# Five blocks of a chunked retention layer with their causal halves on partition halves

## Chip, cores and metric

One core of one Trainium2 chip runs the whole kernel. The metric is the device time of one execution in microseconds (us), as the median of the runs shown.

## The reference

Inputs are q, k, v of 4 batches x 8 heads x 768 tokens x 64. For each batch and head a 64 x 64 state is carried along the tokens, `state = gamma_h * state + k_t v_t^T`, and `y_t = q_t . state / 8`. The outputs of the eight heads side by side make 3072 rows of 512. Each row then goes to one of 8 experts: its normalized product with the normalized expert rows, over `tau`, chooses the expert by argmax and gives the gate (softmax). The expert is `relu(x @ w1[e]) @ w2[e]`, with w1 512 x 1024 and w2 1024 x 512, times the gate.

## The kernel before

**Retention in blocks.** A block m is 256 tokens of one batch for all heads; there are 12, three to a batch (c = m mod 3). A block has two halves u of 128 tokens. Scaling q by gamma^t and k by gamma^-t turns the recurrence into plain products: within a half, scores K Q^T under a causal mask, times V; from earlier tokens, q times the summed state. One loop turn of the program, here step m, does:

- `scores` (L381): per half, 8 products of a 64 x 128 key tile with 128 queries (each matmul is two instructions, fp32), into PSUM banks taken in turn by `pt_` (four banks b0 to b3). `masks` (L402) multiplies them by the 0/1 mask on VectorE, two operations of 512 elements a half.
- `inter` (L453): queries times state, for the halves that have a state.
- `state(m + 1)` (L410): keys times values of the next block, added up in PSUM; for c = 2 only the first half is needed. `state_copy` (ScalarE) and `state_sums` (VectorE) bring it to SBUF.
- the router's logits of block m - 1, and the transposes of the next block's keys and queries, in the order k0, q0, q1, k1. Each is copied from PSUM by ScalarE.
- `intra` (L460): masked scores times values, one half after the other. The outputs of half u stand in bank py0 or py1 (for c > 0).
- `take` (L465): ScalarE copies the outputs, three copies.

Values have to lie as 128 tokens of one half on 128 partitions, while they are loaded with two tokens to a partition. `spread_v` (L395) therefore copies them between partition halves, four copies a block: on ScalarE right after `take` of the step before, and on GpSimd for blocks 10 and 11. Keys are not spread: `state` takes them 64 partitions at a time.

**GpSimd** scales keys and queries of block m + 2 in step m (`scale_ahead`, L867; `scale_k`, L347; `scale_q`, L341), four operations, bound behind the first mask of step m. In steps 4 and 7 the queries are bound behind the router's marks (`mark`, at the end of the step) instead. A transpose of queries needs both query scalings.

**The order** on each engine is written out by hand in the loop at L878; the engines work in that order, with semaphores between them. SP issues all plain transfers in order, with eight semaphores in turn, so that an issue also waits for the landing of the one eight before it. In step m it issues q, k and v of block m + 3 and the output rows of block m - 1 (`rows`, four transfers of 32 partitions). k waits for `state(m + 1)`, v for the second transpose of queries. Query, key and scaled tiles have three buffers, value tiles four.

**The router** works in four groups of three blocks. Steps 3, 6 and 9 choose experts (`pick`); steps 4 and 7 (and 9 and 10 for the third group) rank the tokens and make marks for a table of token positions, which a matmul (`table`) gathers in steps 5, 8 and 10. After step 11 the experts run one after the other, with split fp32 products; the rows of the first are gathered from step 10 on.

Of the kernel before, what the change touches and what calls it, by code (L numbers as in the profile page):

```python
# [38 lines left out]
NG = 4  # L39
CAPS = (416, 408, 400, 392, 384, 380, 360, 356)  # L40
# [21 lines left out]
def _layout():  # L62
    at, n = {}, 0
    for name, w in (("tq", NCB * 2 * H), ("tk", NCB * 2 * H), ("e16", NE), ("tok", 3),
                    ("cols", NE * NG), ("high", NB), ("rest", NB), ("edges", NG - 1), ("quarters", Q),
                    ("ovthr", NOV), ("caps", NE), ("order", NE)):
        at[name] = (n, n + w)
        n += w
# [8 lines left out]
def _constants():  # L77
# [16 lines left out]
    put("tk", (g ** -t).reshape(P, -1))  # L94
    put("e16", (np.arange(NE) / 16.0)[None, :])
# [11 lines left out]
    c16 = np.concatenate([p[:, None] < p[None, :], np.broadcast_to(p[None, :], (P, P))], 1)  # L107
# [4 lines left out]
def retention_moe(ctx: ExitStack, tc: tile.TileContext, q, k, v, emb, tau, w1, w2, const, const16, out):  # L112
# [7 lines left out]
    cst16 = cp.tile([P, 2 * P], FP16, name="cst16")  # L120
    tri, iota = cst16[:, :P], cst16[:, P:]
# [193 lines left out]
    for i in range(3):  # L315
        qin.append(wp.tile([P, 2, 8, D], F32, name="whi"))
        kin.append(wp.tile([P, H, 2, D], F32, name="wlo"))
    for i in range(4):
# [5 lines left out]
    xge = ap_.tile([P, len(EROWS), XW], F32, name="xge", bufs=1)  # L324

# [8 lines left out]

    def load_k(m, h=slice(0, H)):
        return load(kin[m % 3], k, m, h)

    def load_v(m, h=slice(0, H)):
        return load(vin[m % 4], v, m, h)
# [11 lines left out]

    kTs, qTs, yTs, Ss, pst, tBs = {}, {}, {}, {}, [None, None], {}
# [5 lines left out]
    def copy_k(m, s, ps, copy=nc.scalar.copy, js=slice(0, KT)):  # L358
        if m not in kTs:
            kTs[m] = ap_.tile([P, KT, 2, 2, 64], F32, name="kT")  # L360
        return copy(out=kTs[m][:, js, :, s], in_=ps.rearrange("p (j u c) -> p j u c", j=KT, u=2)[:, js])
# [29 lines left out]
    vs = {}  # L391

    pms = {}

    def spread_v(m, u, copy=nc.scalar.copy):  # L395

        if m not in vs:
            vs[m] = ap_.tile([P, 2, H, D], F32, name="vs")
        i = [copy(out=vs[m][s * 64:(s + 1) * 64, u], in_=vin[m % 4][u * 64:(u + 1) * 64, :, s]) for s in range(2)]
# [10 lines left out]
    def state(m):  # L410

        if m % NCB == 0:
            for u in range(2):
                pst[u] = bank(f"pst{u}").rearrange("p (j c) -> p j c", j=KT)
        for j in range(KT):
            for sk in range(2):
                for u in range(1 + (m % NCB < NCB - 1)):
                    for a in range(2):
                        r = slice(u * 64, (u + 1) * 64)
                        h = 2 * j + a  # L420
                        i = nc.tensor.matmul(pst[u][a * D:(a + 1) * D, j, :D], ks_r[r, m % 3, sk, h, :], vin[m % 4][r, h, sk, :],  # L421
# [24 lines left out]
    def y_product(m, u, j, a, lhsT, rhs):  # L446
# [4 lines left out]
        nc.tensor.matmul(pys[m][b][o * D:(o + 1) * D, j], lhsT, rhs, start=first, stop=True, skip_group_check=True)  # L451
# [8 lines left out]
    def intra(m, u):  # L460
        for j in range(KT):
# [1035 lines left out]
```

## Time and profile before

| what | us |
|---|---|
| runs shown | 394.85, 393.69, 394.06; median 394.06 |
| profiled execution | 395.05, with a span of 393.3 |
| steps 1, 2, 3 begin | 19.28, 27.59, 35.90 |
| steps 4 to 8 begin | 44.00, 52.52, 61.04, 69.14, 77.66 |
| steps 9 to 11 begin, retention ends | 86.18, 94.84, 103.46, 108.95 |

The span runs from the first to the last instruction; the profiled execution's own time is 1.75 longer. A step begins with its first score product. Engines: PE is TensorE, PEld its weight loads, DVE VectorE, ACT ScalarE, POOL GpSimd, SP the engine that issues transfers ("SPq" its queue). A row of the order of time gives start and length of a run of like instructions, with the idle time of the engine before it and what ended that in brackets. The granted TensorE clock was 1.00 in all stretches before 200 us, its upper level of 2.4 GHz.

### The profile page before, as it was taken

The page shows a single profiled execution, that of the slowest core. Times are in us where ns is not written, and L with a number is a line of the kernel's source. Part 1 is how long each engine was busy: PE and PEld are TensorE (multiplying, and loading weights), DVE is VectorE, ACT ScalarE, POOL GpSimd, SP SyncE. Part 2 cuts the span into 40 slices and gives each one's busy share as a digit, 9 for nine tenths or more (in the row PEclk, how much of TensorE's full clock was granted, in tenths as well). Part 3 has the DMA queues.
Part 4 walks back from the last instruction along what each step waited for, and adds up shares of the span by engine and source line. Part 5 has one row for each costly group of instructions (what it writes and reads, how often), then busy time and mean ns, then how long its engine had stood idle before and what let it go on. Part 6 is the DMA issues. An engine that isn't in the chain of part 4 may idle for free.

```text
span 393.3 us, 9709 instructions
## 1 busy us (share of the span) xinstructions
PE 384.4 (98%) x3750; PEld 356.7 (91%) x3750; DVE 245.8 (62%) x562; ACT 220.4 (56%) x390; POOL 143.2 (36%) x156
## 2 busy tenths in 40 slices
PE   8999999999999999999999999999999999999993
PEld 7888888888889988999999999999899889999971
DVE  4656787679999568617753862775477447576400
ACT  3488787787674266537446653744765545453420
POOL 2865446267646404224402711520481151001131
PEclk9999999999999999999999999999999999999997
DMA  8999989889588796795959778796988688933121
GB/s 228 295 302 260 255 225 295 235 245 239 158 249 234 221 261 208 240 236 204 320 183 249 252 260 182 243 329 194 254 290 299 163 280 249 216 122 95 31 101 52
DMA packets 86471, 88.03 MB, mean 224 GB/s; under 512 B 9184, under 2 KB 65120, under 8 KB 86416
## 3 DMA queue, kind: packets, MB, share of 16 engines
q1 hardware_dynamic: 81936, 74.32, 66.8%
q0 software_dynamic: 4304, 12.93, 9.9%
q8 instruction: 31, 0.51, 0.6%
q14 instruction: 24, 0.20, 0.2%
q10 hardware_dynamic: 176, 0.07, 0.1%
HBM read 65.00 MB, written 18.43 MB: 212 GB/s over the span
## 4 chain that ended last, share of the span: by engine, by line
PE 80%; DMA 6%; issue 5%; SPq 3%; POOL 2%; DVE 2%; POOLq 0%; ACT 0%
PE pst L247 10%; PE py L451 9%; PE b L247 9%; PE py L1143 8%; PE py L247 7%; PE b L387 6%; PE b L1143 5%; PE pst L1143 4%; PE b L1187 4%; PE py L1187 4%; PE pst L421 3%; PE b L356 3%; PE b L374 3%; SPq L1155 3%; DMA xd<-x 2%
## 5 line engine op out<-in xcount | busy, mean ns | idle before, releaser
L233 DVE TENSOR_TENSOR wlo<-raw,whi 128x1024 fp32r<-128x1024 f32 x60 | 73.0, 1220 | 17.7 <-ACT whi L228 12.2
L1169 POOL DMA_INDIRECT out_dram<-og,si x28 | 30.3, 1082 | 124.8 <-ACT og L1162 74.0
L228 ACT CAST whi<-raw 128x1024 fp32r<-128x1024 f32 x64 | 66.1, 1042 | 0.4 <-DMA raw<-in_moe_w_dram 0.3
L664 POOL DMA_INDIRECT xr<-xd,gi x24 | 30.6, 1276 | 21.0 <-issue 19.5
L1123 DVE STREAM_TRANSPOSE xt<-xg 128x384 f32<-128x384 f32 (+1 forms) x28 | 15.7, 578 | 35.5 <-DMA xg<-xs 35.5
L407 DVE TENSOR_TENSOR pm<-b,mask 128x512 f32<-128x512 f32 x48 | 29.8, 683 | 12.8 <-PE b L387 12.8
L247 PE MATMUL pst<-xh,whi 128*128 128x380 f32 (+7 forms) x96 | 32.1, 334 | 0.0
L247 PE MATMUL pst<-xh,wlo 128*128 128x380 f32 (+7 forms) x96 | 32.0, 333 | 0.0
L247 PE MATMUL pst<-xl,whi 128*128 128x380 f32 (+7 forms) x96 | 31.9, 333 | 0.0
L350 POOL TENSOR_TENSOR hl<-wlo,cst 128x512 f32<-128x512 f32 x22 | 22.5, 1042 | 20.2 <-DVE pm L407 13.0
L1116 ACT CAST xh<-xt 128x408 fp32r<-128x408 f32 (+6 forms) x28 | 14.2, 510 | 25.5 <-DVE xt L1123 25.2
L345 POOL TENSOR_TENSOR hh<-whi,cst 128x512 f32<-128x512 f32 x22 | 22.5, 1044 | 13.6 <-issue 13.6
L273 POOL TENSOR_TENSOR r<-r,half 128x4 f32<-128x4 f32 (+1 forms) x9 | 9.0, 999 | 50.6 <-DVE r L272 50.6
L247 PE MATMUL b<-xh,whi 128*128 128x408 f32 (+7 forms) x80 | 26.8, 335 | 0.0
L247 PE MATMUL b<-xl,whi 128*128 128x408 f32 (+7 forms) x80 | 26.7, 333 | 0.0
L247 PE MATMUL b<-xh,wlo 128*128 128x408 f32 (+7 forms) x80 | 26.6, 332 | 0.0
L247 PE MATMUL py<-xh,whi 128*128 128x288 f32 (+7 forms) x80 | 26.3, 329 | 0.0
L247 PE MATMUL py<-xl,whi 128*128 128x288 f32 (+7 forms) x80 | 26.3, 328 | 0.0
L247 PE MATMUL py<-xh,wlo 128*128 128x288 f32 (+7 forms) x80 | 26.2, 328 | 0.0
L387 PE MATMUL b<-qT,kT 64*128 64x128 f32 x384 | 25.2, 279 | 0.5 <-DVE hl L350 0.5
L253 ACT ACTIVATE hh<-pst 128x380 fp32r<-128x380 f32 (+7 forms) x24 | 11.6, 484 | 24.1 <-PE pst L247 24.1
L387 PEld LDWEIGHTS b<-qT,kT 64*128 64x128 f32 x384 | 22.5, 187 | 2.7 <-issue 1.2
(260 smaller groups left out, 1041.8 us busy)
## 6 DMA issues: line engine op xcount, KB each, us to landing
raw<-in_moe_w_dram SPq DMA_DIRECT2D x60, 512.0 KB
whi<-in_q_dram SPq DMA_DIRECT2D x24, 256.0 KB
wlo<-in_k_dram SPq DMA_DIRECT2D x11, 512.0 KB
xd<-x SPq DMA_DIRECT2D x44, 128.0 KB
xs<-xr SPq DMA_DIRECT2D x6, 768.0 KB
whi<-in_v_dram SPq DMA_DIRECT2D x6, 512.0 KB
wlo<-in_v_dram SPq DMA_DIRECT2D x6, 512.0 KB
xg<-xs SPq DMA_DIRECT2D x16, 192.0 KB
```

Source lines behind the costliest of these rows:

```text
L228: nc.scalar.copy(out=hv, in_=rv)
L233: i = eng.tensor_tensor(out=lv, in0=rv, in1=hv.bitcast(F32), op=ALU.subtract)
L247: nc.tensor.matmul(acc[:, :w], a[:, f], x[:, kt, cols], start=(n == 0), stop=(n == 3 * KT - 1))
L345: return eng.tensor_tensor(out=qs_r[:, m % 3, :, a], in0=qin[m % 3][:, a], in1=w, op=ALU.mult)
L350: return eng.tensor_tensor(out=ks_r[:, m % 3, s, h], in0=kin[m % 3][:, h, s], in1=w[:, h], op=ALU.mult)
L387: nc.tensor.matmul(psc[a][:, j], kTs[m][a * D:(a + 1) * D, j, u].rearrange("p s c -> p (s c)"), q_cols(m, a, j, u), start=True, stop=True, ...
L407: o.append(nc.vector.tensor_tensor(out=pm, in0=psc[a], in1=w, op=ALU.mult))
L451: nc.tensor.matmul(pys[m][b][o * D:(o + 1) * D, j], lhsT, rhs, start=first, stop=True, skip_group_check=True)
L664: return nc.gpsimd.indirect_dma_start(out=xr[:n, j, :], out_offset=None, in_=xd[:rows_, :], in_offset=bass.IndirectOffsetOnAxis(ap=gi[:n, ...
L1143: nc.tensor.matmul(acc[:, :c], a[:, f], x[:, kt, :c], start=(n == 0), stop=(n == 3 * FT - 1))
L1169: i = nc.gpsimd.indirect_dma_start(out=out[:, :], out_offset=bass.IndirectOffsetOnAxis(ap=si[:n, e, j:j + 1], axis=0), in_=og[:n, j, :], i ...
L1187: nc.tensor.matmul(acc[:s, :], x[:, kt, at], a, start=(n == 0), stop=(n == 3 * FT - 1))
```

## The change

It concerns blocks 4, 5, 7, 8 and 10 (`CAUSAL`). Quarter n = 2u + f of 64 tokens is the earlier (f = 0) or later (f = 1) half of half u. Keys and values of these blocks are loaded by quarters, 32 partitions each, in four transfers instead of one; quarter (u, f) goes to 32 partitions of partition half f xor u. Each partition holds two tokens.

- **Keys:** `own_k` scales the token that already lies right, for all 128 partitions; `other_k` scales the other one, 32 partitions at a time, into the neighbouring 32 partitions. That is six operations on GpSimd where there were two.
- **Values:** the same move by `spread_v` (four copies of 32 partitions; ScalarE). It is done one step earlier for all blocks, after `take` of step m - 2; for block 10 it is no longer on GpSimd. The values live in `vx`, three buffers, for all blocks; a causal block's load waits for the values of the block three before it, and is issued at the end of step m.
- **Scores:** `split_scores` does, for each quarter of keys, all 128 queries (f = 0) or only the 64 later ones (f = 1), as 64 x 64 tiles in a written order of the quarters. The zeroed quarter (later keys, earlier queries) is neither computed nor read.
- **Masks:** `split_masks`, four operations of 256 elements a half instead of two of 512, with two new fp16 masks.
- **Values' products:** first the later queries, all 128 keys; then the earlier queries, 64 keys. Both halves u in each.
- **State:** 128 keys a product, half as many products; it stands behind the transposes now, ahead of `intra`.
- Keys of block m + 3 are issued with the queries, behind the first mask. In step 9 the output rows of block 8 and a state sum change place. The router's marks get tiles of their own.

```diff
+CAUSAL = (4, 5, 7, 8, 10)
...
+    vx = [hp.tile([P, H, 3, D], F32, name="xh"), hp.tile([P, H, 3, D], F32, name="xl"),
+          ap_.tile([P, H, 3, D], F32, name="vx", bufs=1)]
...
+    def quarters(src, m, dst):
+        b, c = divmod(m, NCB)
+        o = []
+        for n in range(4):
+            u, f = divmod(n, 2)
+            r = (f ^ u) * 64 + u * Q
+            t = c * T2 + n * 64
+            o.append(nc.sync.dma_start(out=dst(u, slice(r, r + Q)),
+                                       in_=src[b, :, t:t + 64, :].rearrange("h (p s) d -> p h s d", s=2)))
+        return o
...
+            return quarters(k, m, lambda u, r: kin[m % 3][r])
...
+            return quarters(v, m, lambda u, r: vx[m % 3][r, :, u:u + 2])
...
+    def own_k(m, u):
+        return nc.gpsimd.tensor_tensor(out=ks_r[:, m % 3, u], in0=kin[m % 3][:, :, u], in1=weights_k(m, u, slice(0, P)), op=ALU.mult)
+
+    def other_k(m, u, f, eng):
+        r = f * 64 + u * Q
+        o = f * 64 + (1 - u) * Q
+        return eng.tensor_tensor(out=ks_r[o:o + Q, m % 3, u], in0=kin[m % 3][r:r + Q, :, 1 - u],
+                                 in1=weights_k(m, 1 - u, slice(r, r + Q)), op=ALU.mult)
...
+    def split_scores(m):
+        psc = [[pt_().rearrange("p (j g q) -> p j g q", j=KT, g=NQ) for a in range(2)] for u in range(2)]
+        for turn in ((0, 0, 0), (0, 1, 0), (0, 1, 1), (0, 0, 1), (0, 1, 2), (0, 1, 3), (0, 0, 2), (1, 0, 0),
+                     (0, 0, 3), (1, 0, 1), (1, 1, 0), (1, 1, 1), (1, 0, 2), (1, 1, 2), (1, 1, 3), (1, 0, 3)):
+            u, f, j = turn
+            n = f ^ u
+            part = LATER if f else slice(0, Q)
+            for a in range(2):
+                nc.tensor.matmul(psc[u][a][n * 64:(n + 1) * 64, j, :, part], kTs[m][a * D:(a + 1) * D, j, u, n],
+                                 q_cols(m, a, j, u)[:, :, part], start=True, stop=True, skip_group_check=True)
+        return psc
...
+            for r, part in ((slice(0, P), LATER), (slice(u * 64, u * 64 + 64), slice(0, Q // 2))):
+                wr = w[r, :, part].unsqueeze(1).broadcast_to([r.stop - r.start, KT, NQ, Q // 2])
+                o.append(nc.vector.tensor_tensor(out=t[r, :, :, part], in0=psc[a][r, :, :, part], in1=wr, op=ALU.mult))
...
+        for f in range(2):
+            r = f * 64 + u * Q
+            o = f * 64 + (1 - u) * Q
+            i.append(copy(out=x[o:o + Q, :, 2 * u], in_=x[r:r + Q, :, 1]))
...
+        if m in CAUSAL:
+            for u in range(1 + (m % NCB < NCB - 1)):
+                for j in range(KT):
+                    for a in range(2):
+                        h = 2 * j + a
+                        nc.tensor.matmul(pst[u][a * D:(a + 1) * D, j, :D], ks_r[:, m % 3, u, h, :], vx[m % 3][:, h, 2 * u],
...
+            part = slice(0, Q // 2) if u else LATER
+            for j in range(KT):
+                for a in range(2):
+                    for n in range(2):
+                        r = slice(n * 64, n * 64 + 64) if u else slice(0, P)
+                        y_product(m, n, j, a, vx[m % 3][r, 2 * j + a, 2 * n],
+                                  pms[a, n][r, j].rearrange("p (g q) -> p g q", q=Q)[:, :, part], part)
...
+            elif keys:
+                for u in range(2):
+                    after(own_k(m + 2, u), i)
+                for u in range(2):
+                    for f in range(2):
+                        after(other_k(m + 2, u, f, nc.gpsimd), i)
...
         if m and m + 3 < NM:
-            for j in load_q(m + 3):
+            o = load_k(m + 3)
+            for j in (*load_q(m + 3), *(o if m + 3 in CAUSAL else [o])):
                 after(j, i)
...
-            if nxt:
-                i = state(m + 1)
+            if nxt and m + 1 not in CAUSAL:
+                state(m + 1)
                 state_copy(m + 1)
-                if m + 3 < NM:
-                    after(load_k(m + 3), i)
...
+                if m + 1 in CAUSAL:
+                    state(m + 1)
+                    state_copy(m + 1)
+                    state_sums(m + 1)
                 intra(m, 0)
...
         take(m)
-        if m < NM - 2:
-            if m < NM - 3:
-                spread_v(m + 1, 0)
-                spread_v(m + 1, 1)
+        if m + 3 in CAUSAL:
+            load_v(m + 3)
+        for n in range(m + 2 if m else 1, m + 3 if m < NM - 3 else 0):
+            spread_v(n, 0)
+            spread_v(n, 1)
```

## Rows read from the trace of the kernel before

**Rows 1.** Page, part 1: busy time, share of the span, instructions, by engine.
```profile
PE 384.4 (98%) x3750; PEld 356.7 (91%) x3750; DVE 245.8 (62%) x562; ACT 220.4 (56%) x390; POOL 143.2 (36%) x156
```

**Rows 2.** Busy time by step; columns: stretch, length, engines, clock, DMA share, GB/s.
```profile
19.28:27.59 8.31, 8.31 (x155) 7.37 (x154) 5.09 (x11) 6.96 (x13) 6.81 (x7) 1.00 1.03 310
...
44.00:52.52 8.52, 8.52 (x161) 7.57 (x161) 5.48 (x16) 6.91 (x12) 2.04 (x2) 1.00 0.95 252
...
61.04:69.14 8.10, 8.10 (x179) 7.09 (x178) 6.22 (x17) 6.12 (x11) 4.05 (x4) 1.00 1.09 295
...
94.84:103.46 8.62, 8.62 (x162) 7.65 (x161) 8.34 (x27) 6.29 (x10) 3.85 (x6) 1.00 0.82 188
```

**Rows 3.** Chain that ended last, in order of time: start, us, what.
```profile
37.89 0.60 PE py L451 x16
38.48 0.93 PE pst L421 x64
...
44.00 1.99 PE b L387 x32
45.98 1.03 PE py L451 x32
47.02 0.92 PE pst L421 x32
47.94 0.57 PE b L498 x8
48.51 0.59 PE b L356 x4
...
50.62 1.90 PE py L451 x32
...
99.94 0.25 PE b L620 x6
```

**Rows 4.** VectorE in order of time, steps 4 and 5: start, us.
```profile
48.95 0.39 DVE L434 TENSOR_TENSOR s<-pst,tB 128x256 f32<-128x256 f32 x1
...
53.43 1.06 DVE L610 TENSOR_SCALAR xh<-cst,low 128x128 f16<-128x128 f16 x6
...
54.41 2.48 DVE L407 TENSOR_TENSOR pm<-b,mask 128x512 f32<-128x512 f32 x4
```

**Rows 5.** GpSimd in order of time, steps 3, 5 and 9.
```profile
38.12 2.04 POOL L350 TENSOR_TENSOR hl<-wlo,cst 128x512 f32<-128x512 f32 x2 [4.44 <-DMA wlo<-in_k_dram]
...
54.98 2.04 POOL L345 TENSOR_TENSOR hh<-whi,cst 128x512 f32<-128x512 f32 x2 [6.99 <-issue]
...
92.12 2.59 POOL L399 COPY vs<-whi 64x512 f32<-64x512 f32 x4
```

**Rows 6.** GpSimd by groups of instructions: busy us, mean ns, idle before.
```profile
L345 POOL TENSOR_TENSOR hh<-whi,cst 128x512 f32<-128x512 f32 x22 | 22.5, 1044 | 13.6 <-issue 13.6
...
L399 POOL COPY vs<-whi 64x512 f32<-64x512 f32 x6 | 3.7, 609 | 0.3
```

**Rows 7.** ScalarE in order of time, steps 1 and 5.
```profile
21.11 2.52 ACT L399 COPY vs<-wlo 64x512 f32<-64x512 f32 x4
24.47 0.58 ACT L361 COPY kT<-b 128x512 f32<-128x512 f32 x1 [0.83 <-ACT vs L399]
...
25.97 0.62 ACT L361 COPY kT<-b 128x512 f32<-128x512 f32 x1
...
52.57 1.17 ACT L473 COPY yT<-py 64x512 f32<-64x512 f32 x2 [0.29 <-PE py L451]
```

**Rows 8.** VectorE in order of time, steps 9 and 10.
```profile
93.96 0.20 DVE L567 TENSOR_TENSOR rs<-b,oh 128x48 f32<-128x48 f32 x1
...
98.59 1.35 DVE L610 TENSOR_SCALAR xh<-cst,low 128x128 f16<-128x128 f16 x6
```

**Rows 9.** SP's queue in order of time: issues of keys and of weights.
```profile
31.60 0.40 SPq L328 DMA_DIRECT2D wlo<-in_k_dram  x1
...
88.79 4.85 SPq L201 DMA_DIRECT2D raw<-in_moe_w_dram  x8
```

More of the change, by code (lines that the diff above doesn't have):

```diff
@@ L106, in _constants @@
     put("order", np.arange(NE)[None, :])
-    c16 = np.concatenate([p[:, None] < p[None, :], np.broadcast_to(p[None, :], (P, P))], 1)
+    n = np.arange(P)
+    seen = [64 * (blk // 2 ^ u)[:, None] + (2 * row + blk % 2)[:, None] <= (n // Q + 4 * (n % Q))[None, :] for u in range(2)]
+    c16 = np.concatenate([p[:, None] < p[None, :], np.broadcast_to(p[None, :], (P, P)), *seen], 1)
     return c.astype(np.float32), np.ascontiguousarray(c16.astype(np.float16))
@@ L119, in retention_moe @@
     cst2 = cp.tile([P, _CW - _C1], F32, name="cst2")
[L120 to L121 removed]
+    cst16 = cp.tile([P, 4 * P], FP16, name="cst16")
+    tri, iota = cst16[:, :P], cst16[:, P:2 * P]
     ident = cp.tile([P, P], F32, name="ident")
@@ L317, in retention_moe @@
         kin.append(wp.tile([P, H, 2, D], F32, name="wlo"))
+    vat = {m: i % 4 for i, m in enumerate(m for m in range(NM) if m not in CAUSAL)}
     for i in range(4):
@@ L450, in y_product @@
         begun.add((m, b, o))
-        nc.tensor.matmul(pys[m][b][o * D:(o + 1) * D, j], lhsT, rhs, start=first, stop=True, skip_group_check=True)
+        t = pys[m][b][o * D:(o + 1) * D, j].rearrange("p (g q) -> p g q", q=Q)[:, :, part]
+        nc.tensor.matmul(t, lhsT, rhs, start=first, stop=True, skip_group_check=True)
     def inter(m):
@@ L868, in scale_ahead @@
         if m + 2 < NM:
-            for s in range(2 * keys):
-                after(scale_k(m + 2, s), i)
+            if keys and m + 2 not in CAUSAL:
+                for s in range(2):
+                    after(scale_k(m + 2, s), i)
+            elif keys:
[4 more added lines that the diff above has]
+                        after(other_k(m + 2, u, f, nc.gpsimd), i)
             for s in range(2 * queries):
@@ L936, in retention_moe @@
             if urgent:
-                rows(m - 1, x=rows_turn(m - 1, (1,), x))
+                rows(m - 1)
             if nxt:
-                if m < NM - 3:
+                if m + 1 not in CAUSAL and m < NM - 3:
                     state_sums(m + 1)
@@ L956, in retention_moe @@
                 i = transpose_q(m + 1, 1)
-                if m + 3 < NM:
+                if m + 3 < NM and m + 3 not in CAUSAL:
                     after(load_v(m + 3), i)
```

58 lines of the change are left out of this document (38 added, 20 removed).

## The prediction, made before the changed kernel was run

> **What bounds the kernel now.** I read the busy shares first, then the busy time by step, the chain that ended last, and the single engines' order of time. TensorE is busy 98% of the span; VectorE 62%, ScalarE 56%, GpSimd 36% [rows 1]. By step, TensorE has no gap in the four retention steps shown, while VectorE fills 8.34 of 8.62 us in step 10 and ScalarE 6.96 of 8.31 in step 1 [rows 2]. So matmul time saved is saved only where the next engine's list still ends first. The chain runs through TensorE in the retention steps, with no wait between its pieces [rows 3].
>
> Two prices come out of the chain. The products with the state run as 64x64 tiles, four side by side: 32 instructions take 1.03 us, 16 take 0.60 [rows 3]. Sixteen more are four more in a row on each tile, so a 128-column instruction costs 0.43/4 = 0.107 us and entering the shape costs 0.60 - 0.43 = 0.17. The state's 64 instructions of 64 columns, same shape, take 0.93: 16 in a row at 0.107/2 give 0.86. I use 0.107, 0.053 and 0.17. "Sn" is the start of step n.
>
> **The change, part by part.**
> *Scores* of a causal block: 1.99 us now [rows 3]. New, each tile has 4 products (8 instructions) of 128 and 4 of 64 columns: 8 x 0.107 + 8 x 0.053 = 1.28; the written order makes a tile wait once for 0.11: 1.39. With 0.17 behind an ordinary block's values, 1.56 (blocks 4, 7, 10), otherwise 1.45 with 0.06 of pipeline edge (5, 8). At two tiles side by side it would be 2.57, the bound above. I take four, as the products with the state show. Those follow in the same shape, so 1.03 becomes 0.87.
> *Values*: 1.90 now. Later queries: 16 in a row x 0.053 = 0.86; earlier ones, four tiles: 0.43 + 0.17. Sum 1.46, or 1.62 where no state product of their shape stands ahead.
> *State*: 128 rows at a time, 16 x 0.053 + 0.17 = 1.02 for 0.93; for blocks 5 and 8, which need one half only, 0.43 + 0.17 = 0.59 for 0.92. Behind it the values enter their shape free (-0.17).
> By step: 3, 6, 9 save 0.08 each; 4 and 7 save 0.43 + 0.16 + 0.33 + 0.44 = 1.4 each; 5 and 8 save 0.54 + 0.16 + 0.28 = 1.0 each; 10 saves 0.87. **TensorE: 5.9 us less.** Steps 4 and 5 would last 7.1 and 7.5 where they now last 8.52 each.
>
> What takes it back, in order:
> *ScalarE, step 1.* Step 0 now spreads two blocks' values instead of one: four more copies, 2.52 us [rows 7]. The idle 0.83 before the key copy at 24.47 goes; the copies that ended at 25.97 + 0.62 = 26.6 end at 28.3. The scores of step 2 need them and stood at 27.59: **0.8 lost**.
> *Output copies.* Ordinary blocks finish one bank of outputs half-way through their values, so ScalarE's first copy (0.58) ends before the step and the other two 1.17 + 0.1 after the step's start, at 52.52 [rows 3, 7]. A causal block finishes both banks at the end: 0.1 + 0.58 + 1.17 + 0.05 = 1.9 after S5. The products with the state arrive at 1.45, do one bank's first few, and wait: **0.45 lost in each of steps 5 and 8**. Before scores of 1.99 it costs nothing; that margin is 0.1.
> *VectorE.* Four masks take 2.48, 0.62 apart for 512 elements; 256-element operations take 0.39 to 0.41 singly, 0.35 in a row [rows 4]. Eight masks: 2.83, +0.35 a causal step. Step 4's list (masks, router transpose, ranks, output transposes, state sum, marks) ends at 53.43 + 1.06, S4 + 10.5, now [rows 4]; VectorE is idle for 3.0 of the 8.52 us of step 4 [rows 2], and as TensorE comes earlier some of that closes: I get S4 + 9.5. Step 5's masks then start 2.4 after S5; each bank is free as TensorE comes to it. Cost 0, and if that cover goes, some 0.5 a step.
> *GpSimd* is the term that decides. Two scalings take 2.04 us, 1.02 each [rows 5]. A causal block has six for the keys, two over 128 partitions and four over 32, and two for the queries. No row has a product over 32 partitions. The nearest is the copy over 64 between partition halves: 0.61 long, four in 2.59, one after the other [rows 5, 6]. Bounds: 0.26 (a quarter's share) to 1.02 and a gap of 0.1. I take 1.02, because the copies show no overlap and all partitions go in parallel anyway. So 8 x 1.02 = 8.16 a block, where it was 4.08.
> In steps 4 and 7 the queries are scaled behind the marks. Mark end S4 + 9.5, the 0.5 seen between 54.49 and 54.98, and 2.04 give S4 + 12.05 = S5 + 4.95, about when TensorE turns block 6's queries: no loss. Behind it block 7's keys end at S5 + 11.05 and its queries at S5 + 13.1. Step 5 lasts 7.5 + 0.45; step 6 turns queries after 1.99 + 0.60 + 0.57 + 0.59 = 3.75, at S5 + 11.7: **1.4 lost**. Block 8's end 8.16 later, at S5 + 21.25. Step 6 is 8.1 long [rows 2], less 0.08, plus the 1.4; step 7 turns queries after 1.56 + 0.87 + 0.57 + 0.59 = 3.6, at S5 + 20.95: **0.3 lost**. Step 9 repeats step 6 with block 10: **1.4 lost**. Behind the waiting turn stand the key copies, the state and all of the next step on TensorE.
> *Step 10.* TensorE's product with the marks starts at 99.94, just when the marks end (98.59 + 1.35) [rows 3, 8]. From the ranks (93.96) VectorE takes 5.98 to there, +0.35 = 6.3. TensorE now needs only 0.86 + 1.56 + 0.87 + 0.93 + 0.57 + 0.59 = 5.4 from its count: **0.9 lost**. That eats step 10's saving.
> *SP and the transfers.* Keys and values come in four issues each instead of one. One issue takes 0.40 for 512 KB; eight of 128 KB take 4.85, 0.6 each [rows 9]. Six more a causal block are 3.6 us on SP, in steps 1, 2, 4, 5 and 7. Keys go out earlier now; causal values go behind the end of step m and are spread at the end of step m + 1, a whole step later. About 2.4 for the four issues and 6.5 for the landing (keys issued at 31.60 were waited for until 38.12 [rows 5, 9], the longest wait of its kind) just fit the 7.1 + 1.9. Cost 0; without that cover ScalarE's queue stands on the spread, 1 to 2 us in each of steps 5 and 6.
> The Trainium skill (DMA: Bandwidth & Descriptors, Rules for kernel authors) says not to split a transfer over partition halves, since the pieces serialize on the same engines: it speaks against this part, and by it the loads gain nothing, as I count.
>
> Sum: -5.9 + 0.8 + 0.9 + 1.4 + 0.3 + 1.4 + 0.9 = -0.2 us. The work after step 11 is unchanged and starts with its end, so it shifts as a whole. Against the profiled execution, 395.05 (span 393.3 and 1.75 around it), that is 394.85; the median of the runs shown is 394.06, 1.0 lower, so 393.9.
>
> **The rivals.**
> *B, the quarter scalings overlap.* The four touch different partitions; if two run side by side they cost 2.04 for 4.08. Block 7's queries are ready by S5 + 11.0, before 11.7, and the 3.1 us of waits for GpSimd go: 390.8. For it: two 1.04 us scalings fill 2.04 [rows 5, 6], so one already starts a little before the other ends. Against: the copies at 92.12 do not overlap.
> Consecutive GpSimd instructions are no barrier between its eight cores, each of which goes on when its own 16 partitions are done, says the Trainium skill (GPSIMD Engine Reference, 2.1 Instruction dispatch). By that rule B holds; the copies' row does not agree.
> *C, slower: GpSimd's instructions wait for each other.* A quarter scaling overwrites what a whole one wrote, so waits may be set between them. 0.1 on each of eight is 0.8 a block: the waits grow to 2.2, 1.1 and 2.2, and 394.1 + 2.2 = 396.3. It decides from about 0.06 an instruction. For it: the copies stand 0.65 apart at 0.61 long. Against: the pairs of scalings show none.
> *D, all engines keep up.* Only ScalarE's 0.8 is lost: 389.0. Against it stands every list above.
> *E, it does not do what it says:* the four tiles run as two, and scores get longer. GpSimd sets the pace in steps 5 to 9 anyway, so the waits shrink by about as much: 394 to 395, counted with A.
>
> **How the numbers follow.** A measurement here tells about 0.3%, 1.2 us. A (the sum, 392.9 to 395.0 by 0.05 us either way on a scaling and 0.5 on VectorE's lists) has 0.40: 0.30 within the bound, 0.06 below, 0.04 above. B 0.29, faster. D 0.07, faster. C 0.24, slower. So faster 0.42, same 0.30, slower 0.28. The likeliest case gives 393.9. The range 390.2 to 396.6 holds A, B and C at the prices worked out, and leaves out D and the far ends.
>
> **What would show it.** Right: scores near 1.4 to 1.6 and values near 1.5; GpSimd back to back from step 5 to 7; TensorE's turns of queries in steps 6 and 9 waiting over 1 us for GpSimd's query scaling; scores of step 2 waiting 0.8 for ScalarE; the marks' product waiting in step 10. Wrong: a quarter scaling well under 1 us, causal steps of 7.1 us with no wait, or a wait for a value load.

## The result, and the profile after

The changed kernel takes 397.81 us in the median of ten runs (395.86 to 399.81), the kernel before 394.56 on the same chip: a ratio of 1.0075, with a 95% interval of 1.0046 to 1.0104. The forecast was 393.9 (390.2 to 396.6): its likeliest single case was no change, while its chances added up to 0.42 for faster, 0.30 for the same and 0.28 for slower. It is slower, by 0.75%, and outside the range. Ratios here leave disturbed runs out, so they differ a little from quotients of medians. The profiled execution took 397.88, its span 396.2.

Page of the changed kernel, part 1, to set beside [rows 1]:

```profile
PE 382.3 (97%) x3942; PEld 352.7 (89%) x3942; DVE 250.2 (63%) x582; ACT 222.2 (56%) x394; POOL 157.4 (40%) x172
```

TensorE is busy 2.1 us less than before and yet the span is 2.9 longer: it stands still for longer. Busy time by step, columns as in [rows 2], for steps 1, 4 to 6 and 9 to 11:

```profile
18.96:28.12 9.16, 8.37 (x155) 7.36 (x154) 5.09 (x11) 8.92 (x17) 6.78 (x7) 1.00 1.07 298
...
44.53:52.30 7.77, 7.64 (x213) 6.57 (x215) 5.93 (x18) 6.31 (x11) 4.62 (x5) 1.00 0.92 243
52.30:61.25 8.95, 8.08 (x267) 7.15 (x256) 7.82 (x25) 6.69 (x12) 6.55 (x7) 1.00 0.79 211
61.25:69.70 8.45, 8.32 (x150) 6.97 (x149) 6.28 (x17) 6.70 (x12) 8.10 (x9) 1.00 0.73 208
...
86.08:95.48 9.40, 8.89 (x156) 7.18 (x158) 7.22 (x23) 6.81 (x12) 8.11 (x8) 1.00 1.00 280
95.48:105.07 9.59, 8.23 (x226) 7.02 (x225) 8.69 (x30) 5.84 (x9) 2.44 (x4) 1.00 0.85 205
105.07:111.57 6.50, 6.10 (x105) 4.74 (x106) 5.61 (x9) 4.32 (x6) 5.23 (x4) 1.00 0.65 180
```

Length minus TensorE's busy time is its standstill: 0.8 us in step 1, 0.9 in step 5, 0.5 in step 9, 1.4 in step 10, 0.4 in step 11. Steps 4 and 7 gain 0.75 each on [rows 2]; steps 5, 6, 9, 10 and 11 lose 0.4, 0.35, 0.7, 1.0 and 1.0. What TensorE waited for between 18 and 118 us (us in total, times, longest):

```profile
PE b L445 <- issue: 1.3, 1, 1.3
PE py L531 <- issue: 1.1, 2, 0.9
PE b L429 <- ACT kT L403: 0.8, 1, 0.8
PE b L416 <- POOL hh L371: 0.5, 1, 0.5
PE py L531 <- ACT yT L562: 0.3, 1, 0.3
```

The kernel before has not one line in this view. The first two say "issue": the profile shows nothing that TensorE waited for. In its order of time they stand inside step 5's products with the state and inside step 10's scores, in the middle of a run of like products:

```profile
52.25 1.57 PE L445 MATMUL b<-qT,kT 64*64 64x128 f32 x64
53.59 0.27 PE L531 MATMUL py<-qT,s 64*64 64x128 f32 x1
54.73 1.11 PE L531 MATMUL py<-qT,s 64*64 64x128 f32 x29 [0.87 <-issue]
...
95.41 1.60 PE L445 MATMUL b<-qT,kT 64*64 64x128 f32 x62
98.36 0.32 PE L445 MATMUL b<-qT,kT 64*64 64x128 f32 x1 [1.35 <-issue]
```

Step 10's stands ahead of the 63rd of 64 score products, which read the same two tiles as those before them. Step 5's may in part be something else: ScalarE copies the outputs of block 4 from 52.48 to 54.26, and in step 8 such copies were waited for (0.28). So the first 0.40 of its 0.87 may be that wait; the rest is not. I call standstills of TensorE without a shown wait, from 18 to 118 us, the gaps. A second difference is SP's queue, to set beside [rows 9] (weights `raw` issued at 88.79 there):

```profile
89.39 2.99 SPq L574 DMA_DIRECT2D xd<-x  x4
92.42 6.04 SPq L208 DMA_DIRECT2D raw<-in_moe_w_dram  x8
98.63 1.86 SPq L574 DMA_DIRECT2D xd<-x  x4
100.59 1.22 SPq L719 DMA_DIRECT2D xd<-zd  x1
```

The router's scores (`xd<-zd`) go out at 100.59, before the change at 95.75; the gather of the first expert's rows needs them.

### The profile page after: what moved, and what is told of

The parts are those of the page before. It is cut to its first block, busy times and chain, and to the rows that moved or that the text cites. A ratio compares the mean times of both kernels' runs of the same rounds, so it can differ in the third digit from the quotient of the medians.

```text
span 396.2 us, 10186 instructions
## 1 busy us (share of the span) xinstructions
PE 382.3 (97%) x3942; PEld 352.7 (89%) x3942; DVE 250.2 (63%) x582; ACT 222.2 (56%) x394; POOL 157.4 (40%) x172
## 4 chain that ended last, share of the span: by engine, by line
PE 60%; DMA 10%; POOL 9%; issue 8%; DVE 5%; SPq 5%; ACT 1%; POOLq 0%; ACTq 0%; DVEq 0%
PE pst L254 10%; PE b L254 9%; PE py L1238 8%; PE py L254 7%; PE b L1238 5%; PE pst L1238 4%; PE b L1282 4%; PE py L1282 4%; DMA wlo<-in_k_dram 4%; POOL hl L389 2%; SPq L1250 2%; PE py L531 2%; POOL hh L371 2%; POOL hl L383 2%; DMA xg<-xs 2%
## 5 line engine op out<-in xcount | busy, mean ns | idle before, releaser
L240 DVE TENSOR_TENSOR wlo<-raw,whi 128x1024 fp32r<-128x1024 f32 x60 | 73.9, 1234 | 21.8 <-ACT whi L235 12.6
L1264 POOL DMA_INDIRECT out_dram<-og,si x28 | 28.5, 1019 | 116.2 <-ACT og L1257 99.2
L752 POOL DMA_INDIRECT xr<-xd,gi x24 | 28.9, 1204 | 21.4 <-issue 19.9
L478 DVE TENSOR_TENSOR pm<-b,mask 128x512 f32<-128x512 f32 x28 | 17.4, 684 | 11.4 <-PE b L429 11.0
L260 ACT ACTIVATE hh<-b 128x408 fp32r<-128x408 f32 (+7 forms) x20 | 9.7, 485 | 25.2 <-PE b L254 20.8
L1238 PE MATMUL py<-hh,whi 128*128 128x408 f32 (+4 forms) x64 | 21.6, 337 | 0.0
L1238 PE MATMUL py<-hl,whi 128*128 128x408 f32 (+4 forms) x64 | 21.4, 335 | 0.0
```

The source lines that it names most:

```text
L240: i = eng.tensor_tensor(out=lv, in0=rv, in1=hv.bitcast(F32), op=ALU.subtract)
L260: nc.scalar.activation(out=hh[:, ft, cols], in_=acc[:, :w], func=AF.Relu)
L478: o.append(nc.vector.tensor_tensor(out=pm, in0=psc[a], in1=w, op=ALU.mult))
L752: return nc.gpsimd.indirect_dma_start(out=xr[:n, j, :], out_offset=None, in_=xd[:rows_, :], in_offset=bass.IndirectOffsetOnAxis(ap=gi[:n, ...
L1238: nc.tensor.matmul(acc[:, :c], a[:, f], x[:, kt, :c], start=(n == 0), stop=(n == 3 * FT - 1))
L1264: i = nc.gpsimd.indirect_dma_start(out=out[:, :], out_offset=bass.IndirectOffsetOnAxis(ap=si[:n, e, j:j + 1], axis=0), in_=og[:n, j, :], i ...
```

## The experiments

Theory S: SP's queue runs late, from the split transfers, and with it the gather that the experts start from. Theory G: the gaps hold the end. Each change is to the changed kernel unless the kernel before is named.

**First four.** e1 issues the weights a step later (`LOADS = (9, 9)` for `(8, 8)`).

> Changed kernel with the first two weight pieces (eight transfers of 128 KB) issued after step 9 instead of step 8, so that the output rows of block 8 and the router's scores (the small transfer from zd) no longer stand behind them on SP. Theory S (SP's queue runs late since the loads are split; the scores' transfer goes out at 100.59 instead of 95.75, and the early gather of the first expert's rows behind it lands at 111.4 instead of 108.3): the scores go out near 95 to 96, the gather lands near 106 to 107, and the time falls by 1.0 to 3.0 us. Theory G (GpSimd's scalings set the pace, the prediction's rival C): the wait is on TensorE ahead of that, the time stays within 0.5 us.

398.84, ratio 1.0100 (1.0060 to 1.0140). The scores went out at 95.37, as before the change, but sixteen weight transfers in a row then landed late, ScalarE stood on them, and TensorE waited 3.3 us for a key copy in step 10. One wait took the place of another, so this decides nothing.

e2 leaves out `other_k`, the scaling of the second token of each key pair:

```diff
-                for u in range(2):
-                    for f in range(2):
-                        after(other_k(m + 2, u, f, nc.gpsimd), i)
```

> Changed kernel without the four 32-partition scalings of a causal block's keys (20 GpSimd operations); half of the keys of these blocks stay unmoved and the output is not the reference's. Theory G: GpSimd's list per causal block falls from 8.5 to 4.1 us, the waits for it in steps 6 and 9 (0.3 and 0.65 us) go, and the time falls by 1 to 3 us. Theory S: SP's queue is as late as before, the scores still go out near 100 us and the gather lands near 111; the time stays within 0.6 us of the changed kernel.

1078.71 in all, ratio 2.73: with wrong keys the tokens choose other experts, and what follows the retention is another program. Up to there the trace can be read: no wait for GpSimd, step 9 at 84.9 (86.08 with the scalings), the early rows' transposes at 109.47 (111.50). With the scalings this point comes 2 us later, but not by them alone: e2 has no gap of 0.5 us either.

e3 takes block 10 out of `CAUSAL` and leaves out the sums of block 10's state.

```diff
-CAUSAL = (4, 5, 7, 8, 10)
+CAUSAL = (4, 5, 7, 8)
```

> Changed kernel with only blocks 4, 5, 7 and 8 causal; block 10 is done as before the change. Its keys and values are two issues again instead of eight, just ahead of the weights and the scores. Theory S: SP is about 3 us less late there, the scores go out near 97 and the time falls by 1.5 to 2.5 us, near the kernel before. Theory G: the wait of step 9 goes, but so does step 10's saving of 0.9 us: the time falls by 0 to 0.8 us. Theory I (TensorE runs out of instructions in step 10, a wait of 1.4 us behind nothing that the profile shows): that wait goes, 1 to 1.5 us.

1043.08, ratio 2.64, for the same reason. Its retention has four gaps, 2.8 us in all, and ends no earlier than in the changed kernel. e8 does it with the sums.

e4 is the kernel before, with nothing changed but the loads of keys and values of the five blocks, in four pieces of 32 partitions:

```diff
+        for n in range(4):
+            t = c * T2 + n * 64
+            o.append(nc.sync.dma_start(out=dst[n * Q:(n + 1) * Q],
+                                       in_=src[b, :, t:t + 64, :].rearrange("h (p s) d -> p h s d", s=2)))
```

> Kernel before the change with one thing added: keys and values of blocks 4, 5, 7, 8 and 10 are loaded in four transfers of 32 partitions each, in the places and at the times of the whole ones. Theory S: SP's queue gets late as in the changed kernel, the scores go out at 98 to 101 us instead of 95.75, and the kernel is slower by 1.0 to 3.0 us though nothing but transfers is changed. Theory G: within 0.5 us of the kernel before.

398.95, ratio 1.0112 (1.0041 to 1.0182), with no gap. So the split by itself costs some 4 us in the order of before. Its path, as the trace has it: keys land late, GpSimd's spreads move into step 10 and stand beside VectorE's marks, the table's products wait 1.4 us for those, and after these waits the granted clock falls to 0.79 from 104 to 112 us, where it was 1.00.

**SP relieved in the changed kernel.** e5 issues the causal values from ScalarE; e6 also loads the keys in three pieces.

```diff
-            return quarters(v, m, lambda u, r: vx[m % 3][r, :, u:u + 2])
+            return quarters(v, m, lambda u, r: vx[m % 3][r, :, u:u + 2], nc.scalar)
```

> The changed kernel with the 20 quarter transfers of the values of blocks 4, 5, 7, 8, 10 issued from ScalarE's queue, after its output copies, not from SP's. Theory S (the changed kernel loses because SP's queue issues late: rows of block 7 at 89.39 against 85.58 before, the scores' transfer at 100.59 against 95.75, and the early gather lands at 111.38 against 108.31, so the first expert product starts 2.6 us late): each step's four issues took 1.9 to 3.4 us of SP, so the scores' transfer goes out near 97, the gather lands 2 to 3 us earlier and the time falls by 1 to 3 us, unless the 2 us that ScalarE now issues delay its copies. Theory G (the gaps of TensorE without a shown wait, 1.4 us in step 10 and 0.9 in step 11, hold the end): the gather comes earlier, but the retention still ends near 111.5 and the time stays within 0.5 us.

> As the kernel before it, and the keys of the five blocks in three transfers in place of four (rows 64 to 127 hold tokens that lie in one piece): SP then issues one transfer more than before the change for each such block, not six. Theory S: the scores' transfer goes out by about 96, as before the change, and the time is 2 to 3.5 us under the changed kernel's, at or under the kernel before. Theory G: within 0.5 us of the changed kernel.

e5: 399.77, ratio 1.0134 (1.0074 to 1.0194). The scores went out at 97.53, three us earlier, as S wanted, but the time did not fall: TensorE now waited 1.8 us for ScalarE's key copies. e6: 400.85, 1.0147 (1.0105 to 1.0189); its profiled execution took 404.67, 3 us more than any other, so its waits are not used. S fails as the whole cause; these edits cannot say more.

**The gaps moved.** e7 shifts all later TensorE instructions by a warm-up of more and shorter products.

```diff
-W0, WN = 27, 192
+W0, WN = 43, 120
```

> The changed kernel with 172 warm-up products of 120 columns in place of 108 of 192 (20640 columns against 20736), which puts every later TensorE instruction at another place among the packets in which instructions are fetched (256 of them in 16 KB), and computes the same. Theory G: the gaps of TensorE without a shown wait move to other places or vanish (1.39 us in the last scores of step 10, 0.9 us in the values of step 11), and the retention ends up to 2 us earlier or as much later. Theory S: wherever the gaps are, the early gather lands near 111.4 and the time stays within 0.7 us of the changed kernel.

398.68, ratio 1.0099 (1.0071 to 1.0128). The gap of step 10 is gone; others stand at 58.26 (1.16) and 84.06 (0.86). The scores went out at 97.53, three us earlier than in the changed kernel, and the time did not fall.

e8 has block 10 as before the change, sums and all.

> The changed kernel with block 10 treated as before (blocks 4, 5, 7, 8 alone changed); the sums of its state stand again ahead of the scores' transfer. Theory S: SP has six issues less (some 3 us) ahead of the rows of blocks 7 and 8 and the scores' transfer, which goes out near 97.5; the time falls by 1 to 2.5 us. Theory G: step 10 has 32 products fewer and its gap may go, but then step 9 does the whole of block 10's state; the time falls only if the gap of 1.4 us vanishes. If block 10 by itself were a gain (0.87 us less TensorE time in step 10 forecast), the time would rise by up to 0.9 us.

396.99, ratio 1.0053 (1.0022 to 1.0085): 0.9 us under the changed kernel by the ratios, whose intervals overlap, with 3.4 us of gaps, the longest (1.77) in step 9, whose block is not cut: a gap can come a step after the products that are.

**More products, but no faster.** e9 is the kernel before with score and value products of the five blocks each cut into two of 64 columns.

```diff
+                for c in range(2) if m in (4, 5, 7, 8, 10) else (None,):
+                    h = slice(0, P) if c is None else slice(c * 64, c * 64 + 64)
+                    nc.tensor.matmul(psc[a][:, j, h], w, x if c is None else x[:, c * 2:c * 2 + 2], ...
```

> The kernel before, with the 32 score products and the 32 value products of blocks 4, 5, 7, 8 and 10 each cut into two of 64 columns: 320 products and 320 weight loads more for TensorE, the same columns, the same data, the same transfers. Theory G (TensorE in the causal steps takes instructions faster than they come in, and stands still for 0.3 to 1.8 us with nothing shown to wait for): such gaps, of which the kernel before shows none between 18 and 113 us, appear here, 1 to 4 us in all, and the time rises by 1 to 3 us. Theory S (only SP's late issues cost): the issues are those of before, no gaps, and the time stays within 0.6 us of before.

406.07, ratio 1.0292 (1.0257 to 1.0326), and no gap, so the number of products alone brings none. TensorE does not wait from 18 to 118 us, so the 11 us are the products themselves; by groups, 43 to 62 us (busy us, mean ns):

```profile
L391 PE MATMUL b<-qT,kT 64*128 64x64 f32 x128 | 7.7, 274 | 0.0
```

128 in 7.7 us are 60 ns each, as long as a whole one of 128 columns (32 in 1.99 [rows 3]). Half the columns with the same 128-column weights saves nothing. Step 4's value products, cut in the same way but with weights of 64 columns, took 2.12 us for 1.90. The Trainium skill (TensorE: Matmul & The Clock Gate, LDWEIGHTS) counts a weight load by its columns, which agrees. In its scores this kernel does 17 products a us, no more than before; the cut scores, 64 in 1.60, are 40.

e10 has blocks 4 and 7 alone changed; e11 puts the state products of blocks 6, 9 and 11 ahead of the products with state:

```diff
+            if m in CAUSAL and m + 1 not in CAUSAL:
+                state(m + 1)
+                state_copy(m + 1)
             inter(m)
```

> The changed kernel with blocks 4 and 7 alone changed (5, 8 and 10 as before). In the changed kernel steps 4 and 7 took 7.77 and 7.78 us against 8.52, but steps 5 and 8 took 8.95 and 8.60 against 8.52 and 8.52, and step 10 9.59 against 8.62. If the steps' times add up: 1.5 us less than before, at 393. Theory S: 18 issues fewer on SP than in the changed kernel, 12 more than before; its queue has caught up by the scores' transfer (about 96.5) and the time is 0 to 1 us under before. Theory G: bursts only in two steps; under before by up to 1 us, or over it by up to 1 us if a gap falls into them.

> The changed kernel with the state products of blocks 6, 9 and 11 ahead of the products with state of blocks 5, 8 and 10, so that these no longer stand first after the shortened scores, where they wait for the output copies of the block before. Theory T (the copies' wait costs 0.5 to 1 us in each of steps 5 and 8, and step 10): the gap of 0.28 us in step 8 and the slow stretch around it go, steps 5, 8, 10 are 0.3 to 0.8 us shorter each, and the time falls by up to 1.5 us. Theories S and G: what is won in steps 5 and 8 is waited for later, and the time stays within 0.7 us of the changed kernel.

e10: 397.28, ratio 1.0101 (1.0037 to 1.0165), steps 4 and 7 at 8.29 each, a gap of 0.69 in step 8, 0.6 of waits for GpSimd. The steps' gains do not add up, which no theory had expected. One reason can be read off: steps 4 and 7 do the state products of blocks 5 and 8, which e10 does whole again (1.1 us in step 4, where the changed kernel takes 0.5). e11: 398.81, 1.0121 (1.0060 to 1.0181): the wait behind the output copies went, and 1.6 us of waits for GpSimd stood in the trace where 0.5 had.

**The runs that decide.** e14 computes the zeroed quarter again; transfers, scalings, spreads and order stay.

```diff
+        for u in range(2):
+            for j in range(KT):
+                for a in range(2):
+                    nc.tensor.matmul(psc[u][a][:, j], kTs[m][a * D:(a + 1) * D, j, u].rearrange("p n c -> p (n c)"),
+                                     q_cols(m, a, j, u), start=True, stop=True, skip_group_check=True)
```

> The changed kernel with the zeroed quarter computed again: 32 score products of 128 columns, four whole masks and 32 value products in each of the five blocks; transfers, scalings, spreads and order stay those of the changed kernel. TensorE has 0.6 us of scores and 0.35 us of values more in each of five steps, 4.75 us in all, and VectorE 0.6 us less in each. Theory G (the shortened products use up instructions faster than they come in): no gaps without a shown wait between 18 and 113 us, and the time rises by 0 to 2.5 us only. If such gaps have nothing to do with the products' pace, they stay and the time rises by 3 to 5 us.

395.46, ratio 1.0004 (0.9974 to 1.0033). TensorE has some 4 us more to do (by the starts of the runs in the two traces, 3.1 of scores and 1.0 of values; 4.75 was expected), and the kernel is 2.8 us faster than the changed one (0.71%; the intervals do not overlap). All its waits from 18 to 118 us:

```profile
PE b L429 <- ACT kT L403: 0.8, 1, 0.8
PE b L416 <- POOL hh L371: 0.6, 2, 0.3
```

No gap. The router's scores go out at 96.47, with all the 30 added issues: in the changed order SP can keep up.

e17 has whole scores and cut values; e18 cut scores and whole values, with zeros written by VectorE.

> The changed kernel with whole score products (32 of 128 columns in each of the five blocks); masks and the 64 cut value products stay. TensorE has 0.6 us more in each of five steps than in the changed kernel, 0.35 us less than with whole products. If the cut scores bring the gaps: none here, and the time is 0 to 1.8 us under e14's, at 394 to 395.5. If the cut values bring them: gaps of 0.5 to 3 us without a shown wait, and 396.5 to 399. If it takes both in one step: a few small gaps, and 395 to 396.5.

> The changed kernel with whole value products (32 of 128 columns and 128 rows) and its cut scores; since these leave a quarter of the masked scores unwritten, VectorE writes zeros there (four small instructions more in each of the five blocks). TensorE has 0.35 us more in each of five steps than in the changed kernel. If the cut scores bring the gaps without a shown wait: 0.5 to 3 us of them between 18 and 113 us, and 396.5 to 399. If only scores and values cut together bring them: none, and 394.5 to 396.

e17: 395.77, ratio 1.0021 (0.9993 to 1.0050), no gap; what the cut values save, GpSimd takes back (1.4 us of waits instead of 0.6). e18: 402.37, 1.0174 (1.0146 to 1.0203), no gap either, but the zeros bring waits of their own. By groups from 44 to 112 us, the zeros cost VectorE

```profile
L458 DVE MEMSET pm<- 64x256 f32 x20 | 5.4, 272 | 2.1
```

and TensorE waited 3.0 us for masks and 1.1 for marks. Whether cut scores alone bring gaps stays open; with both cut, gaps of 0.5 us or more stand in ten of twelve traces (not in e1 and e2), with whole scores in none.

These runs also part G from S. From the first score of step 1 to the transposes behind step 11 it is 93.1 us in e7 and 93.2 in e8, and 90.7 in e14 and 90.8 in e17. In all four the router's scores went out within 1.3 us of each other (97.53, 97.72, 96.47, 97.79); the first two have gaps, the last two none.

**The issues by themselves.** e15 is the kernel before, loads whole, plus 30 transfers of 32 rows of 48 bytes on SP.

```diff
+        for n in range(3):
+            o.append(nc.sync.dma_start(out=small[:, z], in_=src[b, n, c * T2:c * T2 + Q, :12]))
```

> The kernel before, its transfers whole, with three more transfers of 32 rows of 48 bytes behind each of the ten loads of keys and values of blocks 4, 5, 7, 8 and 10: as many issues on SP's queue as in the kernel before with split transfers, which took 398.95 against 394.91, but no large transfer in pieces. Theory N (the number of issues in SP's order, each of which waits for the one eight before, is what costs): the rows, the scores' transfer (95.75 before) and the early gather come 3 to 6 us later and the time is 398 to 400. Theory P (pieces of 32 partitions move their bytes more slowly): the time stays within 1 us of the kernel before.

403.16, ratio 1.0154 (1.0090 to 1.0217), and no gap: more issues on SP's queue are enough to cost what the split cost in e4; small pieces are not needed for it. The router's scores went out at 105.87, and TensorE's longest waits were 0.6, 1.2 and 0.8 us, up to 82.5, 94.9 and 108.0. As in e4, part of the time is the clock, granted at 0.62 from 104 to 113 us.

**Mended.** e12 takes four single waits away: block 2's values spread by GpSimd, queries scaled ahead of the second half of the keys, e11's order, keys in three transfers. e13 is that without block 10, e16 that with whole products.

```diff
                 for u in range(2):
                     after(own_k(m + 2, u), i)
-                for u in range(2):
                     for f in range(2):
                         after(other_k(m + 2, u, f, nc.gpsimd), i)
+                    for s in range(2 * queries * (1 - u)):
+                        after(scale_q(m + 2, s), i)
...
+                spread_v(n, u, nc.gpsimd.tensor_copy if (m, n) == (0, 2) else nc.scalar.copy)
```

> The changed kernel with four single waits taken away: block 2's values spread by GpSimd, not ScalarE, in step 0; for blocks 7 and 10, which were waited for in steps 6 and 9, GpSimd scales the queries ahead of the second half of the keys; state products of blocks 6, 9, 11 ahead of the products with state of blocks 5, 8, 10; the keys of the five blocks in three transfers. Theory W (the single waits hold the time): 0.8 us of step 1, 0.3 of step 6, 0.6 of step 9, 0.3 to 0.5 of steps 5 and 8 and some 2 us of SP's issues come back, and the time falls by 1.5 to 3 us, to the kernel before or a little under it. Theory G (TensorE's gaps without a shown wait): at most 1 us comes back, and such gaps stand in its trace.

> The kernel before it with block 10 as before the change (blocks 4, 5, 7, 8 alone changed). Without block 10 the changed kernel took 396.99 against 394.84 of the kernel before. Theory W: 1.5 to 2.5 us less, 394.5 to 395.5, level with the kernel before or under it. Theory G: 396 or more.

> The changed kernel with whole products and the four single waits taken away (the edits of e12 and e14 together). e14's trace still waits 0.8 us in step 1, 0.3 in step 6 and 0.3 in step 9, and its steps 4 and 7 are 0.4 us shorter than before by the smaller state products. Theories G and W together: 1 to 2 us less than e14, 393.5 to 394.5, under the kernel before by 0.5 to 1.5 us, and no gap without a shown wait between 18 and 113 us. If the mending does no more than move the waits: 395 to 396.

e12: 397.44, ratio 1.0022 (0.9990 to 1.0054): the single waits were worth some 2.1 us (0.53%). e13: 396.23, 1.0010 (0.9977 to 1.0044). Both still have gaps, 2.1 and 4.4 us; from e13's order of time:

```profile
75.82 0.52 PE L536 MATMUL py<-pm,xl 128*64 128x64 f32 x12
77.48 1.08 PE L536 MATMUL py<-pm,xl 128*64 128x64 f32 x40 [1.14 <-issue]
...
79.72 0.57 PE L505 MATMUL pst<-wlo,hl 64*64 64x64 f32 x23
82.47 1.35 PE L505 MATMUL pst<-wlo,hl 64*64 64x64 f32 x41 [2.18 <-issue]
```

e16: 394.03, ratio 0.9973 (0.9946 to 1.0000), 0.6 us under the kernel before by the medians: the only version below it, and just at the edge of what can be told. TensorE is busy without a break through all eleven steps, and waits first at the experts:

```profile
PE py L254 <- DVE xh L762: 0.7, 1, 0.7
```

That wait ends at 110.75, where the first expert product of the kernel before stands at 110.83: the retention ends 1.2 us earlier, but the last gathered rows land at 108.77, before the change at 108.31.

| step lengths, us | 1 | 4 | 5 | 6 | 7 | 8 | 9 | 10 | 11 | 1 to 11 |
|---|---|---|---|---|---|---|---|---|---|---|
| before | 8.31 | 8.52 | 8.52 | 8.10 | 8.52 | 8.52 | 8.66 | 8.62 | 5.49 | 89.67 |
| changed | 9.16 | 7.77 | 8.95 | 8.45 | 7.78 | 8.60 | 9.40 | 9.59 | 6.50 | 92.61 |
| e14, whole | 9.18 | 8.08 | 8.52 | 8.64 | 8.08 | 8.52 | 9.20 | 8.54 | 5.45 | 90.62 |
| e16, whole and mended | 8.30 | 8.14 | 8.53 | 8.10 | 8.15 | 8.52 | 8.66 | 8.54 | 5.46 | 88.82 |

**What the gaps are.** The chip fetches instructions by a DMA queue of its own. In the changed kernel, from 95.6 to 97.1 us, just ahead of the gap that ends at 98.36 (queue, kind: packets, MB, share of 16 engines):

```profile
q1 hardware_dynamic: 147, 0.37, 100.5%
q8 instruction: 1, 0.02, 4.9%
```

4.9% of 16 engines for 1.5 us are 1.18 us: one packet, from 95.75 to 96.93. This queue follows TensorE: it brought 30 packets for the 3622 products of e14, 31 for 3750 before, 32 for 3782 in e17, 33 for 3942 in the changed kernel and 34 for 4070 in e9, 118 to 121 products a packet. And in the 12 profiled executions with both products cut there are 21 gaps of 0.5 us or more: each of the 21 ends 1.2 to 1.6 us after the end of a packet. In the gaps shown, 1.43 both times (packets end at 53.30 and 96.93), 1.55 and 1.52 in e13.

A count settles it. A packet has 16,384 bytes. Number all TensorE instructions that the trace records by the order of their starts: the first one after a gap has 2241, 2497, 3009, 3265, 3521, 3777, 4033 or 4289 ahead of it, in all 21 cases 193 more than a multiple of 256. So the gaps stand where one group of 256 instructions ends and the next begins, 64 bytes to an instruction, whatever the products there are. TensorE had run out of instructions and went on when the next packet was in. The eight executions without both cuts (before, e4, e9 and e14 to e18) have no gap between 18 and 118 us. Of the shorter ones, four (0.17 to 0.40 us) stand at such places too; six of 0.3 in step 11, one of them in the changed kernel (110.10), do not and stay unexplained.

Pace in a short run is not enough: the kernel before does the state's 64 products in 0.93 us [rows 3] without a gap. What counts is the time of a group of 256, and when its successor is fetched. In the groups that begin between 44 and 109 us, a group takes 4.90 us or more in the kernel before and 3.41 or more in the changed one. The next packet starts 0.7 us after the group's beginning on average before (at most 2.3), 1.8 in the changed kernel (at most 3.5), takes 0.9 to 1.6 in the changed one, and is used 1.4 after its end at the earliest. Ahead of the gap that ends at 98.36 it started 3.4 late. Why packets start later there stays open. Whole products are not safe by themselves: in e16 one packet started 4.5 late, and another ended only 1.37 before its first instruction ran, just without a gap.

The Trainium skill (Runtime: NRT & Kernel Launch, Instruction fetch mechanics) says that the next page is fetched while the current one runs and that crossing is mostly hidden. In the kernel before the trace agrees. In the changed kernel it does not at two of the twelve crossings between 44 and 109 us.

## Why the prediction was wrong

**The step that failed** is the frame in its first paragraph: "matmul time saved is saved only where the next engine's list still ends first". It lists engines' work and has no price for how fast TensorE is fed; instruction supply is a term put at nothing. The prices of the products were near: in step 5 the products behind the cut scores start 1.34 us after them (52.25 to 53.59; 1.45 forecast), the values took 1.55 in steps 4 and 7 (1.46 forecast) and 1.70, 1.91 and 1.71 in steps 5, 8 and 10 (1.62). But with both products cut TensorE ran out of instructions, and the saving was lost: with the quarter computed and no gap, the same kernel is 2.8 us faster. No rival had this.

By step lengths, steps 1 to 11 last 2.9 us longer where 0.2 less was forecast. The loss sits behind the cut scores: up to the end of the products with the state some 4.4 us are lost in the five steps, by starts of runs (1.2 and 1.6 in steps 5 and 10, with the gaps; 0.55, 0.55 and 0.5 in steps 4, 7 and 8, with the output copies), where the forecast has 0.1. Step 11 adds 1.0, since its values took 2.91 for 1.90, with nothing in the trace to say why. On the other side, some 2.1 of the 3.1 us of waits for GpSimd and the 0.9 for the marks did not come. So the number missed by less than the account did, by luck.

**ScalarE, step 1:** right. 0.8 forecast, 0.8 measured; the longer spread, to set beside [rows 7]:

```profile
20.79 2.54 ACT L464 COPY xl<-wlo 64x512 f32<-64x512 f32 x4
23.36 2.53 ACT L464 COPY vx<-whi 64x512 f32<-64x512 f32 x4
...
27.40 0.61 ACT L403 COPY kT<-b 128x512 f32<-128x512 f32 x1
```

**Output copies:** the mechanism right, two of its places missing. "Ordinary blocks finish one bank of outputs half-way" does not hold for blocks 3 and 6 (c = 0), which write both banks to the end. So steps 4 and 7 lose 0.55 each too (products with the state 1.65 for 1.10), where nothing was forecast. Step 8 loses about what was forecast: what follows its products with the state starts some 1.5 us after them for 0.92 before, 0.28 of it a shown wait. In step 5 the loss lies within the gap.

**GpSimd:** the price right, the waits too long. Groups of instructions from 44 to 95 us, to set beside [rows 6]:

```profile
L389 POOL TENSOR_TENSOR hl<-wlo,cst 32x512 f32<-32x512 f32 x14 | 14.5, 1036 | 1.0
...
L383 POOL TENSOR_TENSOR hl<-wlo,cst 128x512 f32<-128x512 f32 x6 | 6.1, 1045 | 0.0
```

A scaling of 32 partitions takes as long as one of 128, and four take 4.35 one after the other. This is the case taken for A. The last three of the four wait for no semaphore and still start 0.06 to 0.08 after the end of the one before; so rival B, and what it drew from the rule quoted with it (the Trainium skill, GPSIMD Engine Reference, 2.1 Instruction dispatch), do not hold here. But the waits of 1.4, 0.3 and 1.4 came out as 0.1, 0 and 0.5 of idle time (the turns of queries start 0.3, 0 and 0.7 late); step 5 lasted 8.95 and not 7.95, which gave GpSimd that much longer. Rival C (waits between its instructions, 0.05 each) decided nothing.

**VectorE:** cost 0 held, no wait of TensorE for a mask is shown; eight masks took 3.08, not 2.83. **Step 10:** the marks' product did not wait 0.9: the marks ended at 100.77, and TensorE, late by its gap, came at 101.42. **SP:** cost 0 holds in the changed order (e14 is level with before), but not for the reason given: as many issues in the order of before cost 4 us or more (e4, e15). Keys go out earlier in the changed order, behind the first mask; that this is what covers them is likely, but no run shows it alone. In the changed kernel SP was late as well (100.59), and the gather landed at 111.38 when TensorE was ready for it at 111.50: in that execution mending either alone could gain little. Why SP runs late in some executions of this order and not in others (95.4 to 103.5) is open.

## What to carry to other kernels

Cutting work into more and shorter products pays only as long as instructions come in as fast: look for "issue" waits in the middle of a run of like products, count instructions between them, and compare with the same kernel doing the whole work. Waits of different causes stood side by side here, and taking one away alone brought others (e1, e5, e11). Four together were worth some 2.1 us (e12), the whole products 2.8 (e14), and both 4.0 (e16, by the ratios). A split load is paid for in issues on its queue, and the bill can come several steps later (e4, e15).

## What the runs showed that was not expected

- A kernel with some 4 us less work for TensorE was 2.8 us slower than the same one without the saving.
- After running dry TensorE starts again 1.2 to 1.6 us after the end of the instruction packet, in 21 of 21 cases, and each time at a multiple of 256 instructions from the others.
- Thirty transfers of 1.5 KB each, on an otherwise unchanged kernel, cost 1.5% (e15).
- A score product of 64 columns took the 60 ns of one with 128 (e9).
- Twenty zero-writings of 0.27 us on VectorE, which is busy 64% of the span, went with 4.1 us of waits of TensorE for masks and marks that the changed kernel does not have (e18): the share of busy time says little about slack in the steps with marks.
